# Sign bits of float64 weights on ScalarE, and one subtraction for all partitions

## The chip, the cores and the metric

The program runs on one core of a Trainium2 chip. The metric is the device time of one execution in microseconds (us). Before the change it is 1498.42 us, the median of three runs (1497.89 to 1498.97). Five engines matter: PE (TensorE), DVE (VectorE), ACT (ScalarE), POOL (GpSimd) and SP (SyncE, which issues nearly all DMAs).

## The reference, cut to what matters

Three layers follow each other. The first is a delta-rule recurrence over 768 tokens, for 32 pairs of batch and head, with a 48 x 48 state:

```python
for t in range(S):
    y[:, :, t] = einsum('bhd,bhde->bhe', q[:, :, t], state)
    v_old = einsum('bhde,bhd->bhe', state, kt)
    state = state + bt * einsum('bhd,bhe->bhde', kt, vt - v_old)
```

Its output, 3072 tokens by 384, goes through `g = h * sigmoid(1.702 * h)` with `h = x @ w_in` (384 x 2048) and `g @ w_out`. Then come four experts, each `relu(x @ w1[e]) @ w2[e]`, weighted by normalised probabilities. The first layer's weights reach the kernel as float64, because they were scaled by a float64 number; all others are float32.

## The kernel before, in words

**The recurrence** is computed in chunks of 64 tokens, numbered u = 0 to 11, for all pairs at once. A chunk's chain in `queue_chain` is: product with the state (`ks`, L737), subtraction from v (`rest`, L740), product with an inverted triangular matrix for the first 32 tokens (`solve`, L747), a copy to SBUF (L180), product with the cross block (`cross`, L757), subtraction for the second 32 tokens (`rest2`, L762), `solve` again, a copy, then the read of y (`read`, L770), the product for the state (`write`, L775) and its addition (L789, for chunk 0 a copy, L792). The pairs are worked in two halves, and within each half x = 0 and x = 1 lie on different partitions. So `rest2` is issued twice per half: once for partitions 96 to 127, once for 32 to 63. The PSUM tile `ch` that it reads holds on the other partitions what `solve` left there for the first 32 tokens.

The inverted matrices of chunks 0 and 1 are made on DVE, with a last pair of products on PE (`first`, L665, and `second`, L674, with the copy `out1` on ACT between them); those of later pairs of chunks are made on POOL, starting from a transpose on DVE (L562) and ending with one (L594). `queue_g` (L515, L518) and `queue_q` (L448) make products of keys with keys and with queries, masked on DVE (L526, L453); `pq` is the tile of queries.

**The first layer's weights** come in 16 blocks f = 0 to 15 of 128 x 768 float64 numbers, read as pairs of 32-bit words `lo` and `hi`. `queue_w1` turns them into float32 with five instructions a block: `small` on ACT (L261) multiplies `hi`, seen as float32, by 2^-112, which lowers the exponent; `low` (L264) shifts `lo` right by 29; `shift` (L268) shifts `hi` left by 3 and ors it in; `sign` (L272) ors in the sign bit of `hi`, which the shift pushed out. Then `hi()` on ACT (L277) and `lo()` on DVE (L280) split the result into two float32r tiles `w`.

**The first layer** takes tokens in 6 tiles of 512 (two chunks each): per block f nine products L889 into `ph`, a gate on ACT (L992, L994) and DVE (L995), nine products L977 into `px`. Tile 0 is halved for f < 8, tile 1 for all f: the 256 tokens of the first chunk run before those of the second. A half can start when its chunk's y has gone through stage copies (L180), stage DMAs (L853) and a split into `xs` (L180, L883). The experts follow (L889 again, L1091).

**The order of work** is set when the program is built: an `Order` object keeps one clock for each engine and gives each `Task` an engine, a cost in us and a priority. Whenever a big product is issued, `tick` moves time on and issues each task that would be ready. A task less, or a cost changed, therefore moves instructions on every engine. Each engine then runs its list in that order and waits where an input is missing.

Of the kernel before, what the change touches and what calls it, by code (L numbers as in the profile page):

```python
# [149 lines left out]
def delta_attention_moe_moe_kernel(  # L150
# [11 lines left out]
    nc = tc.nc  # L162
# [73 lines left out]
    def queue_w1(f, after):  # L236

        kw = dict(prio=(FIRST_W if f < 2 else EARLY_W if f < N_EARLY else LATE_W) + f / 50, slack=0.5)
        later = {F1 - 1: (wdone.get(0),)}
        cell = {}

        def load():
            if f in (0, F1 - 1):
                t = raw.rearrange("p h c -> p (h c)")
            else:
                t = wp.tile([128, 1536], F32, name="rw", tag="w")  # L250
            dst = t.bitcast(I32) if wide else t
            nc.sync.dma_start(out=dst if wide else dst[:, 0:768], in_=w[f])
            if wide:
                pairs = dst.rearrange("p (n t) -> p n t", t=2)
                cell["lo"], cell["hi"] = pairs[:, :, 0], pairs[:, :, 1]
                cell["t"], cell["top"] = cell["lo"].bitcast(F32), cell["hi"].bitcast(F32)
            else:
                cell["t"] = t[:, 0:768]

        def small():  # L260
            nc.scalar.activation(out=cell["top"], in_=cell["top"], func=AF.Copy, scale=2.0 ** -112)  # L261

        def low():
            nc.vector.tensor_scalar(out=cell["lo"], in0=cell["lo"], scalar1=29, scalar2=None,  # L264
                                    op0=ALU.logical_shift_right)

        def shift():
            nc.vector.scalar_tensor_tensor(out=cell["lo"], in0=cell["hi"], scalar=3, in1=cell["lo"],  # L268
                                           op0=ALU.logical_shift_left, op1=ALU.bitwise_or)

        def sign():
            nc.vector.scalar_tensor_tensor(out=cell["lo"], in0=cell["hi"], scalar=-2 ** 31, in1=cell["lo"],  # L272
                                           op0=ALU.bitwise_and, op1=ALU.bitwise_or)

        def hi():
            W[f] = wp.tile([128, 2, 768], F32R, name="w", tag="w")
            nc.scalar.copy(out=W[f][:, 0, :], in_=cell["t"])  # L277

        def lo():
            nc.vector.tensor_tensor(out=W[f][:, 1, :], in0=cell["t"], in1=W[f][:, 0, :].bitcast(F32), op=ALU.subtract)  # L280

        dep = task(load, "HW", 2.2 if wide else 1.1, (*later.get(f, ()), *after), lat=3.0, prio=50)
        if wide:
            a = task(small, "ACT", 0.83, (dep,), **kw)
            b = task(low, "DVE", 0.6, (dep, begun[0]), **kw)
            c = task(shift, "DVE", 0.88, (a, b), **kw)
            dep = task(sign, "DVE", 0.88, (c,), **kw)
        h = task(hi, "ACT", 0.73, (dep, wdone.get(f - 1)), **kw)
        wdone[f] = task(lo, "DVE", 0.95, (h,), **kw)

# [400 lines left out]
    def queue_chain(u):  # L691
# [27 lines left out]
        for hu in range(2):  # L719
# [37 lines left out]
                    mm(cell["ps"][r + 32:r + 64, i, :], lhsT=G[u][r:r + 32, g, :], rhs=SUv[r:r + 32, g, x, :],  # L757
                       start=True, stop=True, tile_position=(r, r + 32))

            def rest2(x, gs=gs, cell=cell):  # L760
                r = TR[x] + 32
                V.tensor_tensor(out=V2[u][r:r + 32, gs], in0=V2[u][r:r + 32, gs], in1=cell["ps"][r:r + 32],  # L762
                                op=ALU.subtract)

            def read(each=each, cell=cell):
                held["yg"] = cell["yev"]
# [31 lines left out]
        for hs in [halves[0:1], halves[1:2]] if u < 2 else [halves]:  # L798
# [21 lines left out]
            a = task(both("solve", 0), "PE", 0.8 * n, (*bs, invdone[u]), prio=p, can=None if u else room)  # L820
            bs = solved_tasks(0, a)
            a = task(both("cross"), "PE", 0.76 * n, (*bs, *crossed[u]), prio=p)
            bs = [task(lambda x=x, h=h: h["rest2"](x), "DVE", 0.47, (a,), prio=p) for h in hs for x in range(2)]
            a = task(both("solve", 32), "PE", 0.8 * n, bs, prio=p)
            for h in hs:
                solved2[u, h["hu"]] = a
# [362 lines left out]
```

## Time and profile before

| what | value |
|---|---|
| median of three runs | 1498.42 us (1497.89 to 1498.97) |
| profiled execution: time | 1498.39 us |
| profiled execution: span, first to last instruction | 1496.2 us |
| PE busy | 1427.9 us, 95% |
| DVE busy | 648.5 us, 43% |
| ACT busy | 458.9 us, 31% |
| POOL busy | 200.1 us, 13% |

A span is the time between the first and the last instruction of one profiled execution; 2.2 us lie around it. The shares are averages over very different stages: the beginning, in which the recurrence has no other work beside it, the long middle in which chunks and layer run together, and the experts from about 690 us on, in which PE is full.

### The profile page before, as it was taken

The page shows a single profiled execution, that of the slowest core. Times are in us where ns is not written, and L with a number is a line of the kernel's source. Part 1 is how long each engine was busy: PE and PEld are TensorE (multiplying, and loading weights), DVE is VectorE, ACT ScalarE, POOL GpSimd, SP SyncE. Part 2 cuts the span into 40 slices and gives each one's busy share as a digit, 9 for nine tenths or more (in the row PEclk, how much of TensorE's full clock was granted, in tenths as well). Part 3 has the DMA queues.
Part 4 walks back from the last instruction along what each step waited for, and adds up shares of the span by engine and source line. Part 5 has one row for each costly group of instructions (what it writes and reads, how often), then busy time and mean ns, then how long its engine had stood idle before and what let it go on. Part 6 is the DMA issues. An engine that isn't in the chain of part 4 may idle for free.

```text
span 1496.2 us, 30416 instructions
## 1 busy us (share of the span) xinstructions
PE 1427.9 (95%) x13552; PEld 1264.9 (85%) x13552; DVE 648.5 (43%) x1074; ACT 458.9 (31%) x864; POOL 200.1 (13%) x341
## 2 busy tenths in 40 slices
PE   2687998999999999999999999999999999999999
PEld 2677888997888888887999999999999999999998
DVE  6979857456545434332322342222432323423222
ACT  5444443334345233342211131112321112212111
POOL 2019307820270440000000000000000000000000
PEclk8577999999999999999999999999999999999999
DMA  9211021021101100320000020000110000100001
GB/s 328 100 25 36 12 58 27 12 51 58 49 22 27 26 22 18 118 74 0 1 0 1 1 85 0 1 0 1 53 32 0 0 1 21 44 21 22 21 22 43
DMA packets 41331, 53.71 MB, mean 36 GB/s; under 512 B 25712, under 2 KB 29936, under 8 KB 41200
## 3 DMA queue, kind: packets, MB, share of 16 engines
q1 hardware_dynamic: 41008, 51.67, 11.3%
q8 instruction: 106, 1.74, 0.5%
q14 instruction: 25, 0.20, 0.0%
q10 hardware_dynamic: 192, 0.10, 0.0%
HBM read 42.71 MB, written 7.86 MB: 34 GB/s over the span
## 4 chain that ended last, share of the span: by engine, by line
PE 90%; DVE 4%; DMA 2%; issue 1%; ACT 1%; SPq 1%; POOL 1%; DVEq 0%; POOLq 0%; ACTq 0%
PE ph L889 40%; PE po L1091 27%; PE px L977 13%; PE ch L747 2%; PE y L770 2%; PE gp L448 2%; DMA pq<-in_q_dram 2%; PE ch L737 1%; PE ch L775 1%; PE ch L757 1%; PE gp L515 1%; DMA rw<-in_w_dram 1%; SPq L853 1%; DVE pq L453 0%; DVE gh L995 0%
## 5 line engine op out<-in xcount | busy, mean ns | idle before, releaser
L889 PE MATMUL ph<-xs,w 128*128 128x512 f32 (+1 forms) x2808 | 666.7, 380 | 8.2 <-DVE w L280 4.2
L889 PEld LDWEIGHTS ph<-xs,w 128*128 128x128 f32 x2808 | 502.0, 191 | 95.7 <-DVE w L280 4.8
L1091 PE MATMUL po<-w,hh 128*128 128x384 f32 x2304 | 432.8, 336 | 0.0
L1091 PEld LDWEIGHTS po<-w,hh 128*128 128x128 f32 x2304 | 407.6, 188 | 17.1
L1118 DVE SCALAR_TENSOR_TENSOR hh<-ph,hh 128x512 fp32r<-128x512 f32 x192 | 133.0, 693 | 553.9 <-ACT hh L1117 553.9
L1117 ACT ACTIVATE hh<-ph 128x512 fp32r<-128x512 f32 x192 | 115.0, 599 | 632.1 <-PE ph L889 632.1
L977 PE MATMUL px<-gh,w 128*128 128x512 f32 (+1 forms) x1080 | 233.9, 356 | 2.3 <-DVE gh L995 2.2
L977 PEld LDWEIGHTS px<-gh,w 128*128 128x128 f32 x1080 | 179.5, 194 | 31.0 <-DVE gh L995 3.8
L995 DVE TENSOR_TENSOR gh<-ph,gh 128x512 fp32r<-128x512 f32 (+1 forms) x120 | 69.5, 580 | 140.5 <-ACT gh L994 139.5
L992 ACT ACTIVATE ph<-ph 128x512 f32<-128x512 f32 (+1 forms) x120 | 59.4, 495 | 214.0 <-PE ph L889 205.5
L573 POOL TENSOR_TENSOR scr<-scr,itmp 128x30 f32<-128x30 f32 (+9 forms) x150 | 91.9, 612 | 11.8
L571 POOL TENSOR_TENSOR itmp<-scr 128x30 f32<-128x30 f32 (+9 forms) x150 | 84.7, 565 | 11.4
L994 ACT CAST gh<-ph 128x512 fp32r<-128x512 f32 (+1 forms) x120 | 60.2, 502 | 3.8
L180 ACT COPY su<-ch 32x384 f32<-32x384 f32 x73 | 34.4, 471 | 55.2 <-PE ch L747 47.5
L515 PE MATMUL gp<-kt 48*32 48x64 f32 x768 | 29.3, 233 | 20.1 <-ACT kt L180 19.8
L515 PEld LDWEIGHTS gp<-kt 48*32 48x32 f32 x768 | 25.9, 118 | 24.1 <-ACT kt L180 20.9
L1083 DVE TENSOR_TENSOR xs<-x,xs 128x512 fp32r<-128x512 f32 x72 | 45.3, 685 | 2.0 <-ACT xs L1082 2.0
L448 PE MATMUL gp<-pq,kt 48*64 48x64 f32 x768 | 34.1, 255 | 11.4 <-DMA pq<-in_q_dram 10.2
L747 PEld LDWEIGHTS ch<-v,scr 32*32 32x32 f32 x1536 | 36.5, 110 | 9.1 <-issue 4.6
L448 PEld LDWEIGHTS gp<-pq,kt 48*64 48x64 f32 x768 | 31.4, 167 | 14.6 <-issue 10.5
L565 POOL MEMSET scr<- 128x32 f32 x5 | 0.8, 159 | 311.7 <-DVE scr L562 311.7
L747 PE MATMUL ch<-v,scr 32*32 32x48 f32 x1536 | 40.4, 208 | 2.1 <-DVE v L762 1.9
(108 smaller groups left out, 883.7 us busy)
## 6 DMA issues: line engine op xcount, KB each, us to landing
raw<-in_we_dram SPq DMA_DIRECT2D x32, 384.0 KB, 3.0
rw<-in_w_dram SPq DMA_DIRECT2D x14, 768.0 KB, 12.6
k<-in_k_dram SPq DMA_DIRECT2D x12, 384.0 KB, 4.6
pq<-in_q_dram SPq DMA_DIRECT2D x24, 192.0 KB, 4.5
v<-in_v_dram SPq DMA_DIRECT2D x12, 384.0 KB, 3.2
out_dram<-oacc SPq DMA_DIRECT2D x24, 192.0 KB, 1.9
x1d<-raw SPq DMA_DIRECT2D x12, 256.0 KB, 2.1
x<-x1d SPq DMA_DIRECT2D x4, 768.0 KB, 6.5
```

Source lines behind the costliest of these rows:

```text
L448: mm(ps[TR[x]:TR[x] + C, i, :], lhsT=kt[d:d + D, g, :], rhs=pq[d:d + D, g, x, :], start=True, stop=True)
L515: mm(ps[r:r + SB, i, :], lhsT=kt[d:d + D, g, 0:SB], rhs=kt[d:d + D, g, :], start=True, stop=True)
L571: E.tensor_tensor(out=tv, in0=x[:, j:j + 1, j + 1:].broadcast_to([128, m, r]), in1=x[:, 0:m, j:j + 1].broadcast_to([128, m, r]), op=ALU.mult)
L573: E.tensor_tensor(out=x[:, 0:m, j + 1:], in0=x[:, 0:m, j + 1:], in1=tv, op=ALU.add)
L747: mm(cell["ps"][r:r + 32, i, :], lhsT=Tb[u][r:r + 32, g, :], rhs=V2[u][r:r + 32, g, :], start=True, stop=True, tile_position=(r, r))
L889: mm(ps, lhsT=w[:, a, kk * 128:(kk + 1) * 128], rhs=xs[kk][:, b, cs], start=kk == 0 and i == 0, stop=kk == KD - 1 and i == 2)
L977: mm(px[d][:, cs], lhsT=w[:, a, 384 + d * 128:384 + (d + 1) * 128], rhs=gh[:, b, 0:cs.stop - cs.start], start=f == 0 and i == 0 and cs.sta ...
L994: a = task(lambda: nc.scalar.copy(out=hi, in_=ph), "ACT", 0.05 + 0.43 * c, (a,), **kw)
L995: a = task(lambda: nc.vector.tensor_tensor(out=lo, in0=ph, in1=hi.bitcast(F32), op=ALU.subtract), "DVE", 0.07 + 0.53 * c, (a,), **kw)
L1091: mm(po[b], lhsT=hh[:, a, b * 128:(b + 1) * 128], rhs=w[:, c, 384:768], start=f == 0 and i == 0, stop=f == F2 - 1 and i == 2)
L1117: nc.scalar.activation(out=hh[:, 0, :], in_=ph, func=AF.Relu)
L1118: nc.vector.scalar_tensor_tensor(out=hh[:, 1, :], in0=ph, scalar=0.0, in1=hh[:, 0, :].bitcast(F32), op0=ALU.max, op1=ALU.subtract)
```

## The change

One instruction per weight block goes, and one per half of a chunk. The parametric ReLU multiplies a negative input by `alpha` as well: for a positive `hi` the exponent is lowered by 112 as before, for a negative one the result is positive and its exponent is lowered by 112 - 32 = 80 only, so one more exponent bit is set, which `shift` moves into the place of the sign. `rest2` becomes one instruction for all 128 partitions of a half; what it writes on the partitions of the first 32 tokens is not read again.

```diff
-            nc.scalar.activation(out=cell["top"], in_=cell["top"], func=AF.Copy, scale=2.0 ** -112)
+            nc.scalar.activation(out=cell["top"], in_=cell["top"], func=AF.Prelu, scale=2.0 ** -112, alpha=-2.0 ** 32)
...
-        def sign():
-            nc.vector.scalar_tensor_tensor(out=cell["lo"], in0=cell["hi"], scalar=-2 ** 31, in1=cell["lo"],
-                                           op0=ALU.bitwise_and, op1=ALU.bitwise_or)
...
-            c = task(shift, "DVE", 0.88, (a, b), **kw)
-            dep = task(sign, "DVE", 0.88, (c,), **kw)
+            dep = task(shift, "DVE", 0.88, (a, b), **kw)
...
-            def rest2(x, gs=gs, cell=cell):
-                r = TR[x] + 32
-                V.tensor_tensor(out=V2[u][r:r + 32, gs], in0=V2[u][r:r + 32, gs], in1=cell["ps"][r:r + 32],
-                                op=ALU.subtract)
+            def rest2(gs=gs, cell=cell):
+                V.tensor_tensor(out=V2[u][:, gs], in0=V2[u][:, gs], in1=cell["ps"], op=ALU.subtract)
...
-            bs = [task(lambda x=x, h=h: h["rest2"](x), "DVE", 0.47, (a,), prio=p) for h in hs for x in range(2)]
+            bs = [task(h["rest2"], "DVE", 0.47, (a,), prio=p) for h in hs]
```

The planner's list changes from the first weight block on. The changed file's line numbers are lower: L277 there is L280 before, L661 is L665, L670 is L674, L733 is L737, L743 is L747, L758 is L762, L765 is L770, L770 is L775, L878 is L883, L884 is L889, L972 is L977, L990 is L995; L265 and L269 are L264 and L268.

On PE, the end of chunk 0 (both reads of y are `y`; the products `gp<-scr` finish the inverse of chunk 1). Before:

```order
L770 MATMUL y<-pq_78,su 48x64 x16
L775 MATMUL ch_652<-su,k_0_81 48x48 x16
L775 MATMUL ch_673<-su,k_0_81 48x48 x16
L665 MATMUL gp<-scr_100,scr_99 32x16 x64
L770 MATMUL y<-pq_78,su 48x64 x16
L674 MATMUL gp<-scr_98,scr_100 32x16 x64
```

The second read of y stands between the two products of the inverse. Now:

```order
L765 MATMUL y<-pq_78,su 48x64 x16
L770 MATMUL ch_652<-su,k_0_81 48x48 x16
L770 MATMUL ch_675<-su,k_0_81 48x48 x16
L661 MATMUL gp<-scr_100,scr_99 32x16 x64
L670 MATMUL gp<-scr_98,scr_100 32x16 x64
L765 MATMUL y<-pq_78,su 48x64 x16
```

It now stands behind both, and the second of them waits for a copy on ACT.

On DVE, from the split of chunk 0's tokens on (`xs`; `gh` is a gate of the layer, `w` a finished weight block). Before:

```order
L883 TENSOR_TENSOR xs<-stage,xs 128x256 x3
L526 TENSOR_TENSOR scr_100<-gp,scr_100 128x256
L337 STREAM_TRANSPOSE scr_99<-k_3_84 128x512 x2
L180 COPY kt_77<-scr_99 32x16x32
L995 TENSOR_TENSOR gh<-ph,gh 128x256
L180 COPY kt_77<-scr_99 32x16x32
L272 SCALAR_TENSOR_TENSOR rw<-rw 128x768
L995 TENSOR_TENSOR gh<-ph,gh 128x256
L264 TENSOR_SCALAR rw<-rw 128x768
L268 SCALAR_TENSOR_TENSOR rw<-rw 128x768
L272 SCALAR_TENSOR_TENSOR rw<-rw 128x768
L995 TENSOR_TENSOR gh<-ph,gh 128x256
```

Three blocks `w` were finished ahead of this place. Now:

```order
L878 TENSOR_TENSOR xs<-stage,xs 128x256 x3
L269 SCALAR_TENSOR_TENSOR rw<-rw 128x768
L265 TENSOR_SCALAR rw<-rw 128x768
L269 SCALAR_TENSOR_TENSOR rw<-rw 128x768
L990 TENSOR_TENSOR gh<-ph,gh 128x256
L277 TENSOR_TENSOR w<-rw,w 128x768
L265 TENSOR_SCALAR rw<-rw 128x768
L990 TENSOR_TENSOR gh<-ph,gh 128x256
L269 SCALAR_TENSOR_TENSOR rw<-rw 128x768
L277 TENSOR_TENSOR w<-rw,w 128x768
```

Five blocks `w` are finished ahead of it, the last key transposes stand ahead of it too, and no L272 is left.

On PE, where the chain of chunk 2 starts inside the layer's tile 0. Before (ahead of these rows, one 512-token product group of block f = 8):

```order
L889 MATMUL ph<-xs,w 128x512 x9
L977 MATMUL px_1143<-gh,w 128x512 x3
L977 MATMUL px_1144<-gh,w 128x512 x3
L977 MATMUL px_1145<-gh,w 128x512 x3
L889 MATMUL ph<-xs,w 128x512 x9
L977 MATMUL px_1143<-gh,w 128x512 x2
L737 MATMUL ch_2123<-su,kt_76 64x48 x16
```

Now:

```order
L884 MATMUL ph<-xs,w 128x512 x7
L972 MATMUL px_1193<-gh,w 128x512 x3
L972 MATMUL px_1194<-gh,w 128x512 x3
L972 MATMUL px_1195<-gh,w 128x512 x3
L884 MATMUL ph<-xs,w 128x512 x9
L972 MATMUL px_1193<-gh,w 128x512 x2
L733 MATMUL ch_2332<-su,kt_76 64x48 x16
```

Of the L889 groups of tile 0 with 512 tokens, three stood ahead of the chain and five stand there now, and so do the two key products (L515, L518) of chunk 4, which came after the chain's start before.

## Rows read from the trace of the kernel before

**Rows 1.** The page: busy time, share of the span and instructions.

```profile
PE 1427.9 (95%) x13552; PEld 1264.9 (85%) x13552; DVE 648.5 (43%) x1074; ACT 458.9 (31%) x864; POOL 200.1 (13%) x341
```

**Rows 2.** Windows: start:end, length, busy us per engine, PEclk, DMA share, GB/s.

```profile
40.00:83.06 43.06, 31.62 (x1025) 29.07 (x1025) 38.09 (x68) 17.19 (x32) 0.00 (x0) 0.54 0.28 82
83.06:141.49 58.43, 44.31 (x776) 40.49 (x776) 50.46 (x65) 28.06 (x58) 34.22 (x43) 0.79 0.11 24
141.49:213.36 71.87, 71.87 (x1057) 62.32 (x1057) 54.38 (x92) 34.34 (x70) 21.12 (x21) 0.97 0.07 17
213.36:245.00 31.64, 28.31 (x498) 26.58 (x497) 17.77 (x31) 10.54 (x25) 11.64 (x26) 0.89 0.27 76
690.00:1496.20 806.20, 802.55 (x4032) 726.18 (x4031) 247.71 (x381) 168.21 (x285) 0.00 (x0) 1.00 0.05 17
```

**Rows 3.** Groups by line and shape: count, busy us, mean ns, idle before.

```profile
L272 DVE SCALAR_TENSOR_TENSOR rw<-rw 128x768 int32<-128x768 int32 x14 | 14.8, 1057 | 0.2
L272 DVE SCALAR_TENSOR_TENSOR raw<-raw 128x768 int32<-128x768 int32 x2 | 1.9, 952 | 0.0
L762 DVE TENSOR_TENSOR v<-v,ch 32x384 f32<-32x384 f32 x48 | 26.6, 554 | 8.3 <-PE ch L757 7.4
L740 DVE TENSOR_TENSOR v<-v,ch 128x384 f32<-128x384 f32 x22 | 12.1, 552 | 9.4 <-PE ch L737 9.4
L261 ACT ACTIVATE rw<-rw 128x768 f32<-128x768 f32 x14 | 12.3, 903 | 5.8 <-DMA rw<-in_w_dram 5.8
L375 ACT ACTIVATE scr<-k 128x768 f32<-128x768 f32 x11 | 9.3, 846 | 8.8 <-DMA k<-in_k_dram 8.7
```

**Rows 4.** Timelines (start us, us, line) of PE and DVE, end of chunk 0.

```profile
66.48 1.58 PE L665 MATMUL gp<-scr,scr 32*32 32x16 f32 x128 [1.56 <-DVE su L792]
68.00 1.95 PE L770 MATMUL y<-pq,su 128*48 128x64 f32 x32
70.38 1.90 PE L674 MATMUL gp<-scr,scr 32*32 32x16 f32 x128 [0.44 <-ACT scr L180]
79.46 3.67 PE L448 MATMUL gp<-pq,kt 48*64 48x64 f32 x62 [0.87 <-DMA pq<-in_q_dram]
...
63.37 1.83 DVE L421 TENSOR_TENSOR k<-k,scr 128x768 f32<-128x768 f32 x2
```

**Rows 5.** Timeline of PE, end of chunk 1 to the second 256 tokens.

```profile
128.27 1.75 PE L770 MATMUL y<-pq,su 128*48 128x64 f32 x30 [0.18 <-ACT su L180]
136.53 0.44 PE L448 MATMUL gp<-pq,kt 48*64 48x64 f32 x2 [5.06 <-DMA pq<-in_q_dram]
137.89 3.67 PE L448 MATMUL gp<-pq,kt 48*64 48x64 f32 x62 [0.91 <-DMA pq<-in_q_dram]
```

**Rows 6.** Timeline of DVE: the second state subtraction of chunk 1.

```profile
117.69 0.54 DVE L740 TENSOR_TENSOR v<-v,ch 128x384 f32<-128x384 f32 x1
```

**Rows 7.** Timeline of ACT and of the DMA queue: key copies, stage and query loads.

```profile
179.40 2.51 ACT L180 COPY kt<-scr 32x512 f32<-32x512 f32 x4
...
72.15 1.84 SPq L853 DMA_DIRECT2D stage<-scr  x3
74.09 1.28 SPq L434 DMA_DIRECT2D pq<-in_q_dram  x2
130.72 1.82 SPq L853 DMA_DIRECT2D stage<-scr  x3
193.15 5.02 SPq L853 DMA_DIRECT2D stage<-scr  x6
```

**Rows 8.** Timelines of POOL and DVE: end of chunk 2's inverse, and a later one.

```profile
159.50 2.69 POOL L577 TENSOR_TENSOR scr<-scr,bt 128x1024 f32<-128x1024 f32 x1
...
168.87 2.15 DVE L594 STREAM_TRANSPOSE scr<-scr 128x1024 f32<-128x1024 f32 x1
```

**Rows 9.** The chain that ended last: chunk 2's start.

```profile
170.54 2.00 PE ch L737 x64
```

**Rows 10.** Groups: the one table load.

```profile
L897 ACT ACT_TABLE_LOAD x1 | 1.3, 1283 | 0.8 <-PEq L1176 0.8
```

## The prediction

> **What bounds the kernel now.** The page first: PE is busy for 95% of the span [rows 1], so only time in which PE lacks work can be won. The windows show where that is: from 690 us on PE is busy for 802.55 of 806.20 us, and from 141.49 to 213.36 for all of 71.87, while it idles for 11.4 of 43.06 us before 83.06 and for 14.1 of 58.43 us before 141.49. In those two windows DVE is busy for 38.09 and 50.46 us [rows 2]. So I call 40 to 83 stage A, 83 to 141 stage B, 141 to 213 stage C, and ask of each when it ends. Stage A ends when the first 256 tokens of layer one can start, behind a product L448 that waits for query tile `pq` [rows 4]; stage B ends the same way for chunk 1's 256 tokens, with a wait of 5.06 us [rows 5]. What PE has to do afterwards is the same in both kernels, so an end of stage B that comes earlier reaches the end of the program, unless stage C opens a new gap.
>
> **What goes.** Sixteen `sign` instructions took 14.8 + 1.9 = 16.7 us of DVE. The 48 half-wide `rest2` took 26.6 us at 554 ns; 24 take their place on 128 partitions, and L740, the same subtraction from the same kind of PSUM tile on 128 partitions with as many elements each, takes 552 ns [rows 3], so 13.2 us remain and 13.4 go. Together 30 us of DVE. Four signs and the subtractions of chunks 2 to 11 (20 x 0.55 saved) lie after stage B, 15 us in all, where PE is full: those I cost at nothing, the layer's products cover them, and if that cover failed each would be worth its own length at most. The Prelu takes the place of a scaled copy on ACT. No row shows a Prelu; the nearest are that copy (903 ns) and the square of the same size (846 ns) [rows 3], so a function other than a copy need not cost more. I take 903 ns, no change, with 0.06 us less and, as nothing excludes it, twice the time as ends.
>
> **Stage A: 2 us later, though DVE has less to do.** Three signs at 0.96 and two of four half-subtractions at 0.55 go, 4.0 us. But the list also moves. Following the new DVE list with the old durations, the key scaling L421 ends at 62.6 instead of 65.2 [rows 4]; but an L264, two L337 and an L268, 2.9 us by their durations, and one more wait then stand ahead of the first state copies L792, which end at 66.5, hardly later than before. L665 waits for them and so runs at 66.6, as it did [rows 4]. Behind it PE now has L674 and only then the second read of y. L674 waits for a copy on ACT that stands behind seven key copies of 0.62 us [rows 7], the first of which can start at 63.9, and a weight cast of 0.9: 63.9 + 4.3 + 0.9 + 0.4 = 69.5. L674 (1.9) ends at 71.4 and the read (1.95) at 73.3, against 69.95 [rows 4]: 3.3 later. Its copies were held up by a busy ACT until then, and the stage DMAs went out at 72.15 [rows 7]; now they go out at 74.0, 1.9 later, the `pq` load behind them too, and L448. The first 256 tokens start at 85.1 instead of 83.1.
>
> **Stage B: 12 us earlier in all.** Nine signs (8.6 us at 952 ns, 9.5 at 1057 [rows 3]), four of eight half-subtractions (2.2 us) and two whole weight blocks, finished before the stage instead of in it, leave DVE's share of this stage. From the split of chunk 0's tokens (82.3 by the walk) to chunk 1's second state subtraction the new DVE list holds 21 instructions that add up to 15.8 us: 98.1 if it never waited. PE's gates and products hold some of them up, and I come to 101.9, against a subtraction that ended at 118.2 [rows 6]. From there to the last read of y it took 11.8 us (130.0 in [rows 5]); in the new list 24 of the layer's 512-token products (in 256-token halves) stand in this piece instead of 2, 22 x 0.24 = 5.3 us more, less 1.1 for the two subtractions: 16.1, and the read ends at 118. Then the same tail: copies, three stage DMAs, the `pq` load, L448, in all 11.5 us [rows 5, 7]. Stage B ends at 129.5 instead of 141.5: **-12.0**. That PE can do this is close: from 85.1 to 118 it has 33.5 us of products at the pace of its undisturbed pieces.
>
> **Stage C: 2 us given back.** Chunk 2's chain needs the inverse from POOL, whose last instruction ended at 162.2, with the transpose on DVE at 168.87 [rows 8]. POOL starts after L562, which comes 2.4 us earlier (99.4), so the inverse is not 12 us earlier. The new list fits that: five groups of 512 tokens and both key products of chunk 4 come ahead of the chain instead of three groups and none, so that it starts at some 170 to 172, as before at 170.54 [rows 9]. But then less of tile 0 is left to hide the chain's latency. From the last read of chunk 2 to tile 1's first product PE has 21 of the layer's products and three steps of chunk 3's chain left, 4.8 + 5.0 = 9.8 us, while copies (0.75), six stage DMAs (5.02 to issue [rows 7], some 2.2 to land) and the split (1.5) take some 9.5 with no gap anywhere. DVE's list from 127 to that chain adds up to about 39 us, 166 if it never waits. I allow 1 us at each place, +2; the ends are 0 and 8 (those DVE instructions 20% longer; L272's mean is 1057 ns on `rw` beside 952 on `raw` [rows 3]).
>
> **Sum:** -12.0 + 2.0 = -10.0. The profiled execution took 1498.39 us, its span and 2.2 us around it, the median is 1498.42: **1488.4 us**.
>
> A rule weighed here: [rows 3] show that signs on `rw` took 1057 ns on average, with POOL at work beside many of them [rows 2], and 952 on `raw`. The Trainium skill (SBUF — State Buffer, SBUF: two separate sides) says that DVE instructions with two SBUF inputs and GpSimd instructions take a shared pair of ports as an exclusive lock, the loser waiting for the whole instruction. By that rule the nine signs of stage B held POOL up as well, and with them gone the inverse ends earlier; the sum would lose its +2. That is the third rival below.
>
> **Rivals.**
> - *PE, not DVE, sets stage B.* PE was busy for 44.3 of its 58.4 us at a granted clock of 0.79 [rows 2], between 1.2 and 2.4 GHz. If the clock stays there, PE needs 43.3 us (one key product moved ahead) and the wait for `pq` of some 6: 85.1 + 49.3 + 2 of small waits = 136.4, 5 us won, less 1 in stage C: 1494.4. For it: the granted clock was 0.54 and 0.79 where PE idled, 0.97 where it was full [rows 2]. Against it: with the weights ready PE idles less.
> - *Stage C turns the gain round.* The place is the transpose L594 ahead of chunk 2's chain. Each microsecond by which the chain starts after 172 is lost one for one; beyond 185 it has taken back 12 and more, and the kernel is slower. On DVE four masks and L562 of the next pair stand ahead of that transpose now, and these need chunk 4's and 5's keys, which come through DVE. If that list runs 20 us later than my 166, the chain starts at 187, 15 us after 172: -12 + 15 + 1 = +4, 1502.4. For it: a wait here blocks the layer's gates behind it. Against it: it would need every instruction to be half as long again.
> - *POOL is freed.* The inverse ends up to nine signs, 8.5 us, sooner, the +2 goes, and of the 3.3 us that PE idles from 213.36 to 245 [rows 2] half goes too: 1484.8.
> - *The Prelu needs another activation table.* The trace has one load, 1283 ns [rows 10]; the new program has one as well, at its start. If tables had to change at each of the nine runs of Prelu, two loads each would be 23.1 us on ACT: 1511.5 if none were hidden. In a sentence of its own: the Trainium skill (ScalarE: Activation LUTs, What ACT_TABLE_LOAD costs) puts a switch between sets at about 2.66 us with its drain, 24 us by estimate for nine switches; no run here shows one.
>
> **How the numbers follow.** My forecast 0.62; PE sets stage B 0.19; POOL is freed 0.11; stage C turns round 0.06; table loads 0.02. A measurement of this kernel can tell 0.2%, 3 us, from no change. The forecast, POOL's case and most of PE's case (0.16) are faster by more: 0.89. Within 3 us: 0.03 of PE's case and 0.01 of stage C's, 0.04. Slower: 0.07. The range goes from 1483.5 (POOL's case with 1 us more) to 1495.0 (PE's case and the 8 us end of stage C), and leaves out the two slower cases and the edges.
>
> **What would show it.** DVE's groups without L272, with 24 subtractions of 128 x 384 at about 0.55; 16 Prelus of about 0.90 and one table load. PE's second L448 with its wait at about 126 and the second 256 tokens at 129.5; the first at 85.1, later than before. Chunk 2's chain at 170 to 172 with no long wait of PE around 200. It is wrong if stage B ends after 135, if L594 waits for POOL, or if PE idles for more than 4 us in stage C.

## The result, and the profile after

The changed kernel took 1484.18 us (median of 4 runs, 1482.00 to 1484.33) against 1498.18 us (1497.89 to 1498.97): ratio 0.9902, 95% interval 0.9885 to 0.9919, so 14.0 us or 1.0% faster. The forecast was 1488.4. Two further comparisons of the same pair gave 0.9898 (0.9883 to 0.9912) and 0.9905 (0.9889 to 0.9921).

The profiled execution took 1484.33 us with a span of 1482.6, 13.6 less than before. First the page's busy times of the changed kernel and some of its windows (engines in the order PE, PEld, DVE, ACT, POOL, then granted clock and DMA), cut where its own stages A, B and C end, with a piece near 220 us and the rest from 680:

```profile
PE 1420.4 (96%) x13552; PEld 1258.2 (85%) x13552; DVE 619.3 (42%) x1033; ACT 459.8 (31%) x866; POOL 191.9 (13%) x340
```
```profile
40.00:86.55 46.55, 31.78 (x1089) 29.38 (x1089) 39.66 (x72) 24.94 (x45) 0.00 (x0) 0.57 0.28 86
86.55:131.55 45.00, 37.16 (x713) 34.31 (x712) 36.26 (x51) 21.38 (x45) 24.42 (x34) 0.84 0.14 31
131.55:205.24 73.69, 73.12 (x1122) 62.76 (x1121) 49.48 (x86) 31.96 (x66) 51.84 (x88) 0.97 0.09 20
216.00:232.00 16.00, 14.55 (x199) 13.89 (x198) 10.89 (x16) 3.95 (x10) 0.00 (x0) 0.89 0.28 60
680.00:1482.60 802.60, 799.03 (x4017) 723.26 (x4016) 246.90 (x381) 167.45 (x284) 0.00 (x0) 1.00 0.05 17
```

Against [rows 1]: PE is busy for 7.4 us less with the same products, and idle for 6.2 us less; together that is the 13.6. The mean granted clock was 0.974 after 0.970. DVE lost 29.2 us. Stage B is 45.00 us long instead of 58.43 [rows 2], stage A 3.5 us longer. The groups that the change touches, of the changed kernel (busy us, mean ns, idle before):

```profile
L269 DVE SCALAR_TENSOR_TENSOR rw<-rw 128x768 int32<-128x768 int32 x14 | 14.7, 1053 | 0.2
L277 DVE TENSOR_TENSOR w<-rw,w 128x768 fp32r<-128x768 f32 x14 | 14.3, 1022 | 1.3 <-ACT w L274 1.2
L758 DVE TENSOR_TENSOR v<-v,ch 128x384 f32<-128x384 f32 x24 | 13.2, 554 | 14.4 <-PE ch L753 12.0 <-ACT w L274 1.2
```
```profile
L262 ACT ACTIVATE rw<-rw x14: 882/898/920, 19.6 to 52.8; 128x768 f32<-128x768 f32 x14
L262 ACT ACTIVATE raw<-raw x2: 897/900/904, 9.8 to 56.8; 128x768 f32<-128x768 f32 x2
```

24 full subtractions at 554 ns are what 48 half ones had cost each, and the Prelus (second fence: ns min/median/max) take what the scaled copy took [rows 3]. The timeline of the changed kernel at the marks of the forecast (start, us, engine, line; in brackets the idle time before):

```profile
66.61 1.54 PE L661 MATMUL gp<-scr,scr 32*32 32x16 f32 x128 [1.61 <-DVE su L787]
69.87 1.90 PE L670 MATMUL gp<-scr,scr 32*32 32x16 f32 x128 [1.71 <-ACT scr L180]
71.70 1.95 PE L765 MATMUL y<-pq,su 128*48 128x64 f32 x32
74.95 1.84 SPq L848 DMA_DIRECT2D stage<-scr  x3
76.89 1.89 SPq L430 DMA_DIRECT2D pq<-in_q_dram  x2
82.94 3.67 PE L444 MATMUL gp<-pq,kt 48*64 48x64 f32 x62 [0.86 <-DMA pq<-in_q_dram]
86.55 3.78 PE L884 MATMUL ph<-xs,w 128*128 128x256 f32 x16
104.33 0.51 DVE L736 TENSOR_TENSOR v<-v,ch 128x384 f32<-128x384 f32 x1
118.56 1.10 PE L765 MATMUL y<-pq,su 128*48 128x64 f32 x32
126.48 0.44 PE L444 MATMUL gp<-pq,kt 48*64 48x64 f32 x2 [6.82 <-DVE rw L269]
131.55 1.86 PE L884 MATMUL ph<-xs,w 128*128 128x256 f32 x7
153.83 1.92 POOL L573 TENSOR_TENSOR scr<-scr,bt 128x1024 f32<-128x1024 f32 x1
171.91 2.23 DVE L590 STREAM_TRANSPOSE scr<-scr 128x1024 f32<-128x1024 f32 x1
```

The first 256 tokens start at 86.55 (before 83.06, forecast 85.1), the second at 131.55 (141.49, 129.5). So 9.9 us are won at the end of stage B, and 14 at the end of the program. The wait at 126.48 is put down to DVE's L269, which ended long before; it is the load of the queries: the next row of that product, at 127.94, waits another 1.03 us for it by name.

To see where the rest came from I compared the traces at equal work: each kind of PE product counts with its mean spacing in both kernels after 145 us, waits left out (the products of the inverse have none there; what they count as moves the first column by up to some 1 us), and a trace is read at the times at which this sum reaches 30 us (the layer's beginning), 60 (the end of stage B), 140 (the last reads of chunk 3, the end of stage C) and 1000 (the experts). The differences to the profiled execution of the kernel before, in us, for it and for the kernels of the experiments:

```
                                          30      60     140    1000
the change                              +1.6    -9.9    -8.4   -13.5
the change, again                       +0.7   -11.4    -9.6   -15.6
the change, third                       +1.4   -10.5    -8.6   -12.0
new_work_old_order                      -1.1    -6.6    -6.6    -6.6
old_work_new_order                      +5.1    -6.4    +2.1    -6.3
sign_alone                              +1.2    -8.2    -8.1    -9.3
subtract_alone                          -4.9   -14.9   -14.8   -12.9
new_work_subtract_order                 -6.1   -15.1   -15.5   -15.3
gram_behind_layer                       +0.1    -9.4    -7.8   -14.4
stores_on_act                           -2.4    -5.9    -5.9    -7.2
before_stores_on_act                    -0.2    -2.4    -1.7    -1.4
after_stores_on_act                     +0.3   -12.1   -10.3   -17.0
before_queries_on_act                   +2.3    +0.3    +0.1    -3.3
queries_on_act                          +1.4    -9.8    -9.2   -19.2
gram_behind_queries                     +1.8    -8.5    -8.1   -18.8
subtract_order_queries                  -4.2   -13.1   -13.2   -20.1
```

Executions of one kernel differ here by up to 3.7 us at the end, so only larger differences, and rows, are argued from. A mark beside a wait is uncertain by that wait: for old_work_new_order the mark 60 stands just ahead of one of 2.92 us, and set a little later it reads -3.1. The traced execution of that kernel was also a fast one, 1491.58 us where its median is 1494.40, so its last column is about 3 us better than usual. The first line holds the finding: 1.5 us given back in stage C, as foreseen, and then 5.1 won where the forecast had no term at all. The other two executions say 6.0 and 3.4.

### The profile page after: what moved, and what is told of

It is laid out like the page before. It is cut to its first block, busy times and chain, and to the rows that moved or that the text cites. A ratio compares the mean times of both kernels' runs of the same rounds, so it can differ in the third digit from the quotient of the medians.

```text
span 1482.6 us, 30388 instructions
## 1 busy us (share of the span) xinstructions
PE 1420.4 (96%) x13552; PEld 1258.2 (85%) x13552; DVE 619.3 (42%) x1033; ACT 459.8 (31%) x866; POOL 191.9 (13%) x340
## 3 DMA queue, kind: packets, MB, share of 16 engines
q8 instruction: 106, 1.74, 0.5%
## 4 chain that ended last, share of the span: by engine, by line
PE 90%; DVE 2%; DMA 1%; ACT 1%; SPq 0%; issue 0%; DVEq 0%
PE ph L884 40%; PE po L1086 27%; PE px L972 13%; PE ch L743 2%; PE gp L444 2%; PE ch L733 1%; PE y L765 1%; DMA pq<-in_q_dram 1%; PE ch L753 1%; PE ch L770 1%; PE gp L511 1%; SPq L848 0%; DVE w L277 0%; DVE gh L990 0%; DVE scr L479 0%
## 5 line engine op out<-in xcount | busy, mean ns | idle before, releaser
L884 PE MATMUL ph<-xs,w 128*128 128x512 f32 (+1 forms) x2808 | 664.8, 379 | 3.7 <-DVE x L180 2.4
L884 PEld LDWEIGHTS ph<-xs,w 128*128 128x128 f32 x2808 | 499.7, 190 | 90.3 <-issue 2.8
L972 PE MATMUL px<-gh,w 128*128 128x512 f32 (+1 forms) x1080 | 233.5, 356 | 0.6 <-DVE gh L990 0.4
L972 PEld LDWEIGHTS px<-gh,w 128*128 128x128 f32 x1080 | 178.5, 192 | 29.4 <-DVE gh L990 2.0
L990 DVE TENSOR_TENSOR gh<-ph,gh 128x512 fp32r<-128x512 f32 (+1 forms) x120 | 69.5, 579 | 147.7 <-ACT gh L989 146.9
L567 POOL TENSOR_TENSOR itmp<-scr 128x30 f32<-128x30 f32 (+9 forms) x150 | 81.4, 543 | 11.4
L743 PEld LDWEIGHTS ch<-v,scr 32*32 32x32 f32 x1536 | 36.5, 110 | 7.8 <-issue 4.6
L743 PE MATMUL ch<-v,scr 32*32 32x48 f32 x1536 | 40.4, 208 | 0.7 <-DVE pq L449 0.5
L180 ACT COPY kt<-scr 32x512 f32<-32x512 f32 (+1 forms) x60 | 37.0, 617 | 12.0 <-DVE scr L333 11.1
```

The source lines that it names most:

```text
L180: (nc.scalar.copy if e == "ACT" else nc.vector.tensor_copy)(out=out_, in_=in_)
L567: E.tensor_tensor(out=tv, in0=x[:, j:j + 1, j + 1:].broadcast_to([128, m, r]), in1=x[:, 0:m, j:j + 1].broadcast_to([128, m, r]), op=ALU.mult)
L743: mm(cell["ps"][r:r + 32, i, :], lhsT=Tb[u][r:r + 32, g, :], rhs=V2[u][r:r + 32, g, :], start=True, stop=True, tile_position=(r, r))
L884: mm(ps, lhsT=w[:, a, kk * 128:(kk + 1) * 128], rhs=xs[kk][:, b, cs], start=kk == 0 and i == 0, stop=kk == KD - 1 and i == 2)
L972: mm(px[d][:, cs], lhsT=w[:, a, 384 + d * 128:384 + (d + 1) * 128], rhs=gh[:, b, 0:cs.stop - cs.start], start=f == 0 and i == 0 and cs.sta ...
L990: a = task(lambda: nc.vector.tensor_tensor(out=lo, in0=ph, in1=hi.bitcast(F32), op=ALU.subtract), "DVE", 0.07 + 0.53 * c, (a,), **kw)
```

## The experiments

My theory at this point: the freed DVE time shortens stage B whatever the order (theory 1); the rival: the planner's new list does it (theory 2).

**The change taken apart into work and order.** new_work_old_order is the kernel before with the changed instructions in its old list: the sign stays as an empty entry, and the first of the two halves issues the whole subtraction.

```diff
-            nc.scalar.activation(out=cell["top"], in_=cell["top"], func=AF.Copy, scale=2.0 ** -112)
+            nc.scalar.activation(out=cell["top"], in_=cell["top"], func=AF.Prelu, scale=2.0 ** -112, alpha=-2.0 ** 32)
...
         def sign():
-            nc.vector.scalar_tensor_tensor(out=cell["lo"], in0=cell["hi"], scalar=-2 ** 31, in1=cell["lo"],
-                                           op0=ALU.bitwise_and, op1=ALU.bitwise_or)
+            pass
...
             def rest2(x, gs=gs, cell=cell):
-                r = TR[x] + 32
-                V.tensor_tensor(out=V2[u][r:r + 32, gs], in0=V2[u][r:r + 32, gs], in1=cell["ps"][r:r + 32],
-                                op=ALU.subtract)
+                if x == 0:
+                    V.tensor_tensor(out=V2[u][:, gs], in0=V2[u][:, gs], in1=cell["ps"], op=ALU.subtract)
```

old_work_new_order is the changed kernel with the old instructions in its new list: the copy, the sign issued by the entry of the shift, both halves by the one entry of the subtraction.

```diff
-            nc.scalar.activation(out=cell["top"], in_=cell["top"], func=AF.Prelu, scale=2.0 ** -112, alpha=-2.0 ** 32)
+            nc.scalar.activation(out=cell["top"], in_=cell["top"], func=AF.Copy, scale=2.0 ** -112)
...
                                            op0=ALU.logical_shift_left, op1=ALU.bitwise_or)
+            nc.vector.scalar_tensor_tensor(out=cell["lo"], in0=cell["hi"], scalar=-2 ** 31, in1=cell["lo"], op0=ALU.bitwise_and, op1=ALU.bitwise_or)
...
-                V.tensor_tensor(out=V2[u][:, gs], in0=V2[u][:, gs], in1=cell["ps"], op=ALU.subtract)
+                for r in (TR[0] + 32, TR[1] + 32):
+                    V.tensor_tensor(out=V2[u][r:r + 32, gs], in0=V2[u][r:r + 32, gs], in1=cell["ps"][r:r + 32], op=ALU.subtract)
```

> The changed instructions (Prelu, no sign, 24 subtractions on 128 partitions) in the order of the kernel before. Theory 1, the freed DVE time sets stage B, and the new order only costs at stage A and wins late: the first 256 tokens start at 80 to 82 us (83.1 before, 86.6 with the change), the second at 129 to 133 (141.5 and 131.6), the waits of PE for the queries of tile 1 near 232 us stay, and the time is 1486 to 1491. Theory 2, the new order makes the gain: 1494 or more, with the second 256 tokens after 137.

> The instructions of the kernel before (copy and sign, two half subtractions) in the order of the change. Theory 1, freed DVE time: it is no faster than the kernel before, 1496 to 1503, since the signs stand ahead of the state again and the second read of y of chunk 0 is still behind the second product of the inverse; the first 256 tokens start at 88 to 91 and the second at 140 to 146. Theory 2, the order makes the gain: 1484 to 1490, the second 256 tokens before 135.

Measured: the new work in the old order 1492.75 us, ratio 0.9963 (0.9950 to 0.9975); the old work in the new order 1494.40, 0.9978 (0.9966 to 0.9991). Both times lie between the ranges of the two theories, so neither holds alone: the work is worth 0.37%, the order 0.22%, and the two together 1.0%, so some 0.4% comes only when both are there (by the three intervals, give or take 0.25). In the old order the first tokens start at 81.93 and the second at 134.92, a gain of 6.6, and not one microsecond is added after that: -6.6 at 60, 140 and 1000. In the new order with the old work the marks are 90.04 and 135.12, then stage C gives back 8.5 us, and then 8.4 are won late (in an execution 2.8 us below its median). PE and DVE in that kernel's stage C:

```profile
138.61 2.08 PE L884 MATMUL ph<-xs,w 128*128 128x256 f32 x8 [2.92 <-DVE xs L878]
144.71 1.22 PE L972 MATMUL px<-gh,w 128*128 128x256 f32 x8 [0.75 <-DVE gh L990]
150.58 1.22 PE L972 MATMUL px<-gh,w 128*128 128x256 f32 x8 [1.30 <-DVE gh L990]
```
```profile
133.70 1.25 DVE L269 SCALAR_TENSOR_TENSOR rw<-rw 128x768 int32<-128x768 int32 x1
134.99 1.33 DVE L271 SCALAR_TENSOR_TENSOR rw<-rw 128x768 int32<-128x768 int32 x1
136.98 2.36 DVE L878 TENSOR_TENSOR xs<-stage,xs 128x256 fp32r<-128x256 f32 x3
```

A weight's shift and sign (L271 is the sign put back) stand ahead of the split of chunk 1's tokens, and the layer waits for that split. So, by these rows, the new order needs the freed DVE time to get through stage C, and what is won late belongs to the order: it is there in both kernels with the new list and in neither with the old.

**Each part alone, with the list that the planner makes for it.** sign_alone is the change with this taken back; subtract_alone is the kernel before with this alone.

```diff
-            def rest2(x, gs=gs, cell=cell):
+            def rest2(gs=gs, cell=cell):
...
-            bs = [task(lambda x=x, h=h: h["rest2"](x), "DVE", 0.47, (a,), prio=p) for h in hs for x in range(2)]
+            bs = [task(h["rest2"], "DVE", 0.47, (a,), prio=p) for h in hs]
```

> The sign part alone, with the order that follows from it; the subtraction stays in two halves. Of the some 14 us of DVE work that the change takes out up to the end of stage B (9 signs there and 3 ahead of it, 6 halves), the signs are over three quarters. Theory 1: three quarters of the gain, 1486 to 1490. If the subtraction is what counts, since it stands in the chain of each chunk: 1493 or more.

> The subtraction on all partitions alone, with the order that follows from it; the signs stay. It takes 3.3 us of DVE out up to the end of stage B, each in the chain of a chunk. Theory 1: 2 to 4 us won, 1494 to 1497. If the chain counts more than the list, 1491 or less.

Measured: 1488.51 us, 0.9941 (0.9925 to 0.9956), and 1486.04, 0.9931 (0.9915 to 0.9947). The second was 8 us off: an edit that takes 13 us of DVE, 3.3 of them up to the end of stage B, won as much as the signs did (their intervals overlap). Its list shows how; PE's timeline of subtract_alone:

```profile
71.67 1.91 PE L674 MATMUL gp<-scr,scr 32*32 32x16 f32 x128 [4.52 <-ACT scr L180]
73.58 0.58 PE L888 MATMUL ph<-xs,w 128*128 128x256 f32 x1
```

The second read of y comes ahead of both products of the inverse, and the layer ahead of chunk 2's query product. The layer starts at 73.58, 9.5 us before that of the kernel before.

**The new work in that list**, the sign kept as an empty entry with its cost:

```diff
-            dep = task(shift, "DVE", 0.88, (a, b), **kw)
+            c = task(shift, "DVE", 0.88, (a, b), **kw)
+            dep = task(lambda: None, "DVE", 0.88, (c,), **kw)
```

> The changed instructions in the order that the planner made for the subtraction alone: the sign stays in the list as an empty entry with its old cost. Theory 1, removed DVE time is worth some 6 us in whatever order, and orders differ by several us among themselves: 3 to 7 us below the subtraction alone (1486.0), 1479 to 1483. Theory 2, an order is only good with the instructions that its costs describe: no gain over the subtraction alone, 1485 to 1488.

Measured: 1484.55 us, 0.9914 (0.9897 to 0.9931), against 0.9931 for the subtraction alone. Theory 1 asked for 3 to 7 us; the ratios differ by 0.17%, 2.5 us, with an interval of some 3.5 us. So taking 16.7 us of signs out of this list wins nothing that can be told: theory 1 is not borne out, though its lower end is not excluded, and 1484.55 lies just outside the range of theory 2. Stage B ends 0.2 us sooner, and PE waits for weights and queries at the same places, for 1.50 and 5.71 us where it had waited for 1.27 and 6.01:

```profile
108.04 0.38 PE L885 MATMUL ph<-xs,w 128*128 128x256 f32 x1 [1.50 <-DVE w L277]
121.50 0.45 PE L445 MATMUL gp<-pq,kt 48*64 48x64 f32 x2 [5.71 <-DMA pq<-in_q_dram]
```

**Stage A's loss undone.** The changed kernel, with chunk 2's query product held until the layer has begun:

```diff
-                         prio=p + 1, can=lambda: some_free(BANKS, whole))
+                         prio=p + 1,
+                         can=lambda: some_free(BANKS, whole) if u != 2 or od.moe else None)
```

> The changed kernel with one condition added: the query product of chunk 2 on PE may come only after the layer has begun. Theory 1, what the new order lost at stage A is the wait for those queries ahead of the layer (5.6 us): the first 256 tokens start at 78 to 80 us instead of 86.6, and 3 to 6 us of it reach the end, 1478 to 1482. Theory 2, the layer then waits for weights, as PE did for DVE in the kernel before, and nothing is won: 1483 to 1487.

Measured: 1480.75 us, 0.9885 (0.9868 to 0.9902), beside 0.9898 (0.9883 to 0.9912) for the change on the same chip, so no difference that can be told, and neither theory is decided. The change beside it:

> The changed kernel once more, beside the following ones on the same chip. If work and order add up as the two mixed kernels say (6.6 us at equal work by the removed instructions in the old order, 6.3 by the order with the old instructions), 12 to 15 us below the kernel before: 1484 to 1487.

It took 1482.35 us, 15.0 us below the kernel before on that chip: the most that adding up work and order gives. The timeline of gram_behind_layer says what takes the place of the loss:

```profile
80.77 4.46 PE L885 MATMUL ph<-xs,w 128*128 128x256 f32 x18 [3.20 <-ACT xs L180]
118.67 1.95 PE L766 MATMUL y<-pq,su 128*48 128x64 f32 x32 [2.80 <-DVE pq L449]
```

The layer starts 5 us sooner than in the change beside it (85.6 us), and the last read of y then waits 2.80 us for a mask of the queries that came later; the second 256 tokens start at 132.14, no sooner than in the change beside it (130.09).

**The late gain.** The same place in the timeline of the kernel before, and then of the changed kernel:

```profile
218.73 4.62 SPq L963 DMA_DIRECT2D x1d<-raw  x3
223.46 4.72 SPq L853 DMA_DIRECT2D stage<-scr  x6
228.28 1.66 SPq L434 DMA_DIRECT2D pq<-in_q_dram  x2
232.30 0.29 PE L448 MATMUL gp<-pq,kt 48*64 48x64 f32 x2 [2.29 <-DMA pq<-in_q_dram]
```
```profile
212.25 2.45 SPq L958 DMA_DIRECT2D x1d<-raw  x3
216.01 4.56 SPq L848 DMA_DIRECT2D stage<-scr  x6
220.67 1.29 SPq L430 DMA_DIRECT2D pq<-in_q_dram  x2
224.49 0.32 PE L444 MATMUL gp<-pq,kt 48*64 48x64 f32 x2 [0.46 <-DMA pq<-in_q_dram]
```

Before, tile 0's three stores leave SP at 223.35, and chunk 3's six stage transfers start right behind; DVE's copy that the first of them needs had ended at 221.67. With the change the stores are out at 214.70 and the transfers start with the copies, at 216.01. That is 1.8 us of queue, and PE's wait for the queries falls by as much, from 3.33 us (2.29 and 1.04) to 1.45 (0.46 and 0.99). The test moves the stores, the lists stay as they are:

```diff
-                task(lambda d=d: nc.sync.dma_start(out=x1d[t][:, d, :], in_=rawx[:, d * TT:(d + 1) * TT]),
+                task(lambda d=d: (nc.scalar if t == 0 else nc.sync).dma_start(out=x1d[t][:, d, :], in_=rawx[:, d * TT:(d + 1) * TT]),
```

> The changed instructions in the old order, with the three stores of tile 0's result (x1d) issued from ACT's queue instead of SP's. In the old order they stand directly ahead of the six stage transfers of chunk 3 on SP and hold them up by 1.8 us, and the load of the queries and PE's product behind it. Theory 1, this is a part of what the new order wins near 230 us: PE's wait for the queries there falls from 3.7 us to 1.9 or less and the time by 2 to 4 us, to 1489 to 1491. Theory 2, the queue is not what sets that wait: 1492 to 1494, the wait unchanged, or longer if the issues on ACT hold up its copies.

> The kernel before, with the three stores of tile 0's result issued from ACT's queue. Theory 1, the new order wins near 230 us because these stores no longer stand directly ahead of chunk 3's stage transfers on SP: the wait for queries there falls from 3.3 us to 1.5 or less and the time by 2 to 4 us, 0.9973 to 0.9987 of the kernel before. Theory 2, the gain there has another cause: 0.999 to 1.001.

> The same edit in the changed kernel, where the stores have left SP's queue 1 us before the stage transfers want it. Theory 1: no gain, within 1 us of the changed kernel. Theory 2, any relief of SP's queue helps: 2 to 4 us below it.

> The changed kernel beside the three others: 0.989 to 0.991 of the kernel before.

Measured: in the new work in the old order 1489.60 us, 0.9947 (0.9929 to 0.9966) against 0.9963; in the kernel before 0.9987 (0.9975 to 1.0000); in the changed kernel 0.9892 (0.9875 to 0.9909) against 0.9905 (0.9889 to 0.9921) for the change beside it. PE's rows of stores_on_act:

```profile
224.86 0.30 PE L448 MATMUL gp<-pq,kt 48*64 48x64 f32 x2 [0.79 <-DMA pq<-in_q_dram]
226.11 2.16 PE L448 MATMUL gp<-pq,kt 48*64 48x64 f32 x62 [0.95 <-DMA pq<-in_q_dram]
```

The wait falls from 3.71 to 1.74 us there, and from 3.33 to 1.93 in the kernel before: the stores in SP's queue do set about half of it. What that is worth the times cannot tell; every difference lies within its interval, and so does the 1.7 us by which the changed kernel with the edit is below the one beside it. In the kernel before with the edit the granted clock is still 0.80 over 17.00 us (228 to 245), some 3.4 us of lost clock, as much as without it: only the wait itself became shorter.

**The query loads on ACT's queue**, in four kernels:

```diff
-                nc.sync.dma_start(out=pq[DR[x]:DR[x] + D, :, x, :], in_=q[u, x])
+                (nc.scalar if u > 1 else nc.sync).dma_start(out=pq[DR[x]:DR[x] + D, :, x, :], in_=q[u, x])
```

> The changed kernel, its order held, with the loads of the queries of chunk 2 and later issued from ACT's queue; on SP's they stand behind the stage transfers of the chunk before (three of 1.8 us together, six of 4.6). Theory 1, that queue sets PE's three waits for queries in the changed kernel (5.6 us near 82, 7.9 near 127, 1.5 near 225): they fall by 2 to 3 us, 2 to 3 us and to nothing, and most reaches the end: 1476 to 1480. Theory 2, what is won there is given back, or ACT is held up by the loads: 1481 to 1486.

> The same edit in the kernel before. If the 5 us that the forecast lacks were won by a shorter wait for queries near 230 us, the edit takes that wait (3.3 us and the low clock behind it) out of the kernel before as well: 1489 to 1493, and what the change is worth on top of the edit shrinks from 14 us to 9 to 11. If those 5 us came from elsewhere, the distance between the two kernels with the edit stays 14 us.

> The kernel whose query product of chunk 2 stands behind the start of the layer, and the loads of the queries on ACT's queue. Here the first of the three waits is gone already; the other two (7.5 and 1.6 us) should fall by 3 and 1.6: 1475 to 1479 against 1480.8. If not, 1480 to 1484.

> The changed instructions in the order of the subtraction alone, and the loads of the queries on ACT's queue. PE waits for queries there for 6.6 us near 122 and 4.6 us near 315; if these fall by 2 to 3 and 3 to 4.6 us and reach the end: 1477 to 1480 against 1484.6. If not, 1482 to 1486.

> The fastest version once more (changed instructions, the order of the subtraction alone, loads of the queries on ACT's queue): 0.985 to 0.987 of the kernel before, 4 to 7 us below the changed kernel.

Measured: in the change 1479.09 us, 0.9885 (0.9862 to 0.9908); in the kernel before 1494.99, 0.9986 (0.9973 to 0.9998); in gram_behind_layer 1480.27, 0.9888 (0.9871 to 0.9904); in the list of the subtraction alone 1476.60, 0.9859 (0.9837 to 0.9882), and again 1476.68, 0.9857 (0.9839 to 0.9875). Two waits of three did not shrink; PE in queries_on_act:

```profile
81.55 0.45 PE L444 MATMUL gp<-pq,kt 48*64 48x64 f32 x2 [5.07 <-DMA pq<-in_q_dram]
127.09 0.44 PE L444 MATMUL gp<-pq,kt 48*64 48x64 f32 x2 [8.24 <-DVE xs L878]
```

In chunks 0 and 1 half of the stage transfers leave through ACT's queue already, and the load now stands behind those. So the change with this edit came into the range of theory 1 by luck: two of its three steps failed. The third wait, near 225, is gone, and gone from the kernel before too; but there a new one of 2.43 us comes at 328.84, and the time falls by 2 to 3 us only. My expectation that the change would then be worth 9 to 11 us was wrong: it is worth 15.9 by the medians, 15.1 by the ratios. By the rule of that expectation the 5 us that the forecast lacks were therefore not won by that one wait; but the edit helps the changed kernel too, so it does not say what did win them.

In gram_behind_layer the edit changed nothing that can be told. In the list of the subtraction alone it won 0.55% (0.9859 against 0.9914, intervals apart), more than expected: the wait near 122 grew, from 6.6 to 7.7 us, but the one near 314 fell from 4.56 to 0.38, and the low clock behind it went too. The window of new_work_subtract_order, and the same one with the edit:

```profile
312.00:332.00 20.00, 16.73 (x230) 14.34 (x231) 10.33 (x14) 6.15 (x11) 0.00 (x0) 0.83 0.36 99
312.00:332.00 20.00, 19.50 (x313) 16.01 (x312) 15.81 (x29) 9.32 (x17) 0.00 (x0) 1.00 0.25 84
```

The last kernel beats both of the case, 20 to 21 us below the kernel before and 6.2 below the change beside it (1482.90).

## Why the forecast had the sign and missed the size

**What goes** was right: 29.2 us of DVE for 30, the subtraction at 554 ns, the Prelu at 900.

**Stage A** (+2.0) came to +3.5 at the first tokens and +1.6 at equal work (0.7 to 1.6 in three executions), since 64 more products stand ahead of the mark. The read of y ended at 73.65 as worked out (73.3); its copies took 1.3 us to the transfers and not 0.7, and the load of the queries needed 6.05 us to PE's second product against 5.37 before [rows 4, 7].

**Stage B** (-12.0) measured -9.9. Its length was right, 45.0 us for 44.4, so of the miss of 2.1 us stage A's late start is 1.45. Its cause was only half right. In the changed kernel PE has no wait over 0.2 us from 86.55 to 118.56: the stage now ends by PE's own work and the queries, as the first rival had it, though at a granted clock of 0.84 and not 0.79. The experiments correct the rest: at this mark the removed instructions alone win 6.6 us in the old order, the new order alone 6.4, and both together only 9.9, so the two do not add up here. One premise was too narrow as well, that "only time in which PE lacks work can be won": PE's busy time fell by 7.4 us with the same products. In stage B the granted clock rose from 0.79 to 0.84; by estimate from these rows, (1 - 0.79) x 58.43 = 12.3 us were lost to the low clock before and (1 - 0.84) x 45.00 = 7.2 now, so up to 5 of the 13.4 us by which the stage became shorter.

**Stage C** (+2.0) measured +1.5, though chunk 2's chain started later than I said (174.58, not 170 to 172). That the stage can turn round was the second rival, and the old instructions in the new order show it at work: 8.5 us given back, by DVE's list as it said, at the split of chunk 1's tokens and not at L594.

**The step that failed** is "What PE has to do afterwards is the same in both kernels, so an end of stage B that comes earlier reaches the end of the program, unless stage C opens a new gap". By stages B and C the sum would have been -8.4 for -10.0; then came -5.1 (-6.0 and -3.4 in the other executions) for which it had no term. What PE does is the same, but not in what order, and the kernel before still had waits to lose behind 213 us. These I had on the table [rows 2] and used in one rival alone. The layer's end shows in both kernels as the same wait of PE, 2.43 us, up to 689.83 before and 676.30 now. From the end of stage C to there PE idles for 10.2 us before and for 6.6 now (first row before, second with the change):

```profile
213.36:689.83 476.47, 466.31 (x6346) 396.79 (x6345) 232.10 (x399) 187.89 (x384) 135.85 (x249) 0.99 0.15 43
205.24:676.30 471.06, 464.47 (x6281) 395.44 (x6282) 220.76 (x376) 190.50 (x391) 106.71 (x191) 0.99 0.15 42
```

By rows the waits that shrank are 1.9 us for queries near 230; 2.0 us in four short waits of L977 behind 245 us, which have no counterpart; and 0.96 us for a mask of the queries at 340.30, which has none either. The granted clock around the first of them was 0.84 over 21.54 us against 0.89 over 16.00 now, some 3.4 against 1.8 us of clock. The rows of the kernel before for the clock and for L977, a window and PE's group from 241 to 300 us:

```profile
224.00:245.54 21.54, 18.21 (x282) 17.56 (x281) 13.07 (x23) 5.26 (x13) 12.10 (x27) 0.84 0.22 53
```
```profile
L977 PE MATMUL px<-gh,w 128*128 128x256 f32 x179 | 26.6, 287 | 2.1 <-DVE gh L995 2.0
```

Against them stands a new wait for queries in the profiled execution of the change, with its own low clock, 0.91 over 20.00 us or 1.8 us again:

```profile
496.29 2.84 PE L444 MATMUL gp<-pq,kt 48*64 48x64 f32 x62 [1.45 <-DMA pq<-in_q_dram]
490.00:510.00 20.00, 18.55 (x248) 15.31 (x247) 8.30 (x12) 4.86 (x10) 12.55 (x28) 0.91 0.13 24
```

So over the whole stretch the clock won nothing (3.4 us before, 3.6 now). The waits over 0.25 us add up to 9.5 us before and to 6.6 now; the other two executions of the change lack the wait at 496 and have 5.3 and 5.5, with 3.5 and 5.3 us of lost clock. Waits and clock together thus explain some 2.7, 4.1 and 2.1 us of the late gain of 5.1, 6.0 and 3.4; for the remaining 1.3 to 2.4 us no row was found, and that cause stays open.

That SP's queue sets about half of the first wait is shown. That the late gain comes with the order is shown by the two mixed kernels: in the old order the waits of 3.71 us for the queries, 1.45 for L977 and 0.95 for the mask are all there although the signs are gone, and in the new order the old work waits 1.55 us for the queries, not at all for L977 or the mask, and keeps a clock of 1.00 from 225 to 245 us. Each of these waits was not tried on its own.

**The other rivals.** The third, POOL freed, named 1484.8 and so the time, but not by its cause: that is luck. (With 1 us more it gives 1483.8; the range's end of 1483.5 is a little lower.) POOL did become faster: the inverse of chunks 2 and 3 took 51.2 us (104.55 to 155.75) instead of 58.2 (103.99 to 162.19). But the transpose L590 started at 171.91, 16 us after POOL was done, and did not wait for it. The fourth did not come about: the trace has one table load of 1283 ns, as before. (The estimate of 24 us beside it counts nine switches, where nine runs with two loads each are eighteen.)

The rule weighed there is borne out in its mechanism. In a sentence of its own: the Trainium skill (SBUF — State Buffer, SBUF: two separate sides) has DVE instructions with two SBUF inputs and GpSimd's take a shared pair of ports in turn; the trace agrees, with 7.0 us less for the same 62 POOL instructions once the signs are gone, and with 1.25 to 1.33 us for DVE's integer operations beside POOL in the fence above where the undisturbed one took 0.952 [rows 3]. That it is the signs, and not the order or the subtractions, the other runs show: the same 62 instructions took 51.3 us in the old order without the signs (new_work_old_order, 101.35 to 152.66), 51.0 in sign_alone (101.22 to 152.26), which has no signs either, and 56.9 in subtract_alone (93.21 to 150.12), which has them. Only the step from a faster POOL to an earlier end was wrong.

## What to carry to other kernels

Where a planner sets the order, an edit is two changes, fewer instructions and another list, and the second can be as large as the first: cost them apart, and measure them apart by keeping the removed entry in the list with its cost and nothing in it. Mind that the two need not add up: here they gave less than their sum at one mark and, by the times, more at the end. Follow the moved work to the last wait that the old profile shows, not just to the end of the stage that was the bound; each of those waits is a term, even where no instruction of it is touched. And an earlier stage is no gain until the next wait has been looked at: the old instructions in the new order were ahead by 6.4 us at one mark and behind by 2.1 at the next.

## What had not been expected of the hardware

A wait of PE can cost about twice what it shows: around the 3.33 us for queries the granted clock was 0.84 over 21.54 us, some 3.4 us more, as worked out above; the 1.45 us that are left of it with the change came with 0.89 over 16.00, some 1.8 more. Where the wait of 4.56 us near 314 fell to 0.38, the clock from 312 to 332 us went from 0.83 to 1.00. But this is no fixed price. After 1.55 us of waiting in old_work_new_order the clock stayed at 1.00 (225 to 245), while 1.93 us in before_stores_on_act came with 0.80 over 17.00, as much loss as 3.33 us did; and behind the wait of 2.43 us at the end of the layer it was 1.00 in one execution of the change (676.30 to 696.30) and 0.91 in another (672.61 to 692.61 of the second).
